# Reordering the end of a two-layer decode block: row sums, mean and squares, a table gelu, one output turn, and a shorter reciprocal square root

## The chip, the core and the metric

The kernel runs on one core of a Trainium2 chip. The core has a matmul engine (PE, TensorE, with weight loads shown apart as PEld), a vector engine (DVE, VectorE), an activation engine (ACT, ScalarE), POOL (GpSimd, nearly unused here) and SP, which does nothing but issue DMA transfers. Each engine executes its own instructions in program order and waits on semaphores of the others. The metric is the device time of one launch in microseconds.

## The reference

Two rounds of attention and feed-forward, with the same weights and the same key and value caches in both rounds. There are 4 batch rows of one token each, 512 wide.

```python
def _A_ref(x, k_cache, v_cache, wq, wo):          # 32 query heads, 8 KV heads, 4096 keys of 128
    q = (x @ wq).reshape(B, Sq, Hq, Dh).transpose(0, 2, 1, 3)
    k, v = jnp.repeat(k_cache, rep, axis=1), jnp.repeat(v_cache, rep, axis=1)
    p = softmax(einsum("bhqd,bhkd->bhqk", q, k) * Dh ** -0.5)
    o = einsum("bhqk,bhkd->bhqd", p, v)
    return o.transpose(0, 2, 1, 3).reshape(B, Sq, Hq * Dh) @ wo
def _B_ref(x, w_gate, w_up, w_down):              # 512 -> 1792 -> 512, gelu in its tanh form
    return (gelu(x @ w_gate) * (x @ w_up)) @ w_down

x = A_x
x = x + _A_ref(layernorm(x), k, v, wq, wo);  x = x + _B_ref(layernorm(x), wg, wu, wd)
x = x + _A_ref(layernorm(x), k, v, wq, wo);  x = x + _B_ref(layernorm(x), wg, wu, wd)
```

Everything is bf16 in memory. Keys and values of one batch row are 8 MB each.

## The kernel before

The second round of a batch row needs the first round's result of that row only, so the kernel goes row by row: the keys of row b are loaded once and used by both rounds, the values twice (but for two tiles that are kept). All transfers are issued from SP (`dq`). Keys lie in eight buffers of two halves (`KT`), values in seven buffers of 512 KB (`free`) that `load_v` refills as steps give them back.

The order of the work is written out by hand (`manual_schedule`); a call is an instruction at that place of its engine's stream. `attend(b2, b1, ...)` interleaves the second round of row b2 with the first round of row b1. `scores` multiplies q with a key half, `soft` is the softmax, `Values.step` is one value step: 16 matmuls of a value tile with the probabilities, after which the buffer goes back. Behind the scores of the second round the keys of the next row are loaded into the same buffers (L530 to L540), so those loads wait for the scores. `attend_last` is the same for the second round of the last row alone: its value steps, parts of the output projection (`out_proj`) between them, then `y_rows` and `y_select`, which turn the projection's row sums and bring them into columns in a PSUM tile that `out_proj_end` adds to.

Between two `attend` calls stands the feed-forward of the first round, `dense`, for one row: `add_y` (residual), `ln_square` and `ln_center` (a matmul with a matrix of 1/512 gives mean and mean of squares on all partitions; the mean is subtracted), `ln_rstd` (the reciprocal square root on VectorE from an integer start value and two Newton steps), gate and up projections (`ffn_in`) with the 512 wide weights moving, `gelu` (a polynomial on VectorE and a tanh on ScalarE), `gate_up`, and `down`. Then the loop that begins at L708 makes the next norm and q, without the norm's weights: `q_rows`, a turn on VectorE, `q_spread`, and `q_build`, a matmul (`qe`) and a product that writes the operand `qb` of the scores. `fill` is called at fixed places of `dense` and of the loop. For rows 1 to 3 it is a value step of the row before; for row 0 there are none, and it issues idle matmuls (`keep_clock`, L342, into a scores bank) in the numbers of a list, in order of the calls:

```python
            waits = iter((1, 5, 6, 2, 1, 0, 3, 1))
            fill = lambda n: keep_clock(next(waits, 0))
```

The first five numbers belong to `dense`'s calls and to the one between `ln_square` and `ln_center` (L716); then one behind `ln_center`, one behind `q_spread` (L726), one behind `q_build` (L728). Later calls find the list empty and issue nothing.

The second round's feed-forward is made once for all four rows, at the very end (from L745), with the weights standing and 4 columns moving: norm, gate in two halves, `gelu` of each half, up in two halves, `down` (4 columns repeated to 32), the residual into `xo`, four 32x32 turns into `xr`, and the store.

Of the kernel before, what the change touches and what calls it, by code (L numbers as in the profile page):

```python
# [15 lines left out]
P = 128  # L16
# [14 lines left out]
def kernel(  # L31
# [67 lines left out]
    OT2_bf = state.tile([P, Hq, B], BF16, name="OT2_bf")  # L99
    q1_bf = state.tile([P, NG, NK, B], BF16, name="q1_bf")  # L100
    xn_bf = state.tile([P, KD, B], BF16, name="xn_bf")
    xo = state.tile([P, QS], BF16, name="xo")
    xr = state.tile([QS, P], BF16, name="xr")
    qb = state.tile([P, W + NK * 2 * W], BF16, name="qb")

    ROWS = [ps_row.tile([P, 512], FP32, name=f"rows{i}") for i in range(2)]
# [1 line left out]
    ident_bf = const.tile([P, P], BF16, name="ident_bf")  # L108
    mean_f = const.tile([P, P], FP32, name="mean_f")
    magic = const.tile([P, B], I32, name="magic")  # L110
    s32_f = const.tile([P, QS], FP32, name="s32_f")
    t32_bf = const.tile([P, QD, QS], BF16, name="t32_bf")
    amask = const.tile([P, QD], FP32, name="amask")
# [28 lines left out]
    def build_consts():  # L142
        nc.vector.memset(mean_f[:], 1.0 / D)
        nc.vector.memset(magic[:], 0x5F3759DF)
        for r in ROWS:
            nc.vector.memset(r[:], 0.0)
        nc.vector.memset(qb[:], 0.0)
        nc.vector.memset(xo[:], 0.0)
        nc.vector.tensor_reduce(out=amask[:], in_=ident_bf[:].rearrange("p (a i) -> p a i", a=QD),
                                axis=AX.X, op=ALU.max)  # L150
        nc.vector.tensor_reduce(out=s32_f[:], in_=ident_bf[:].rearrange("p (a i) -> p i a", a=QD),
                                axis=AX.X, op=ALU.max)
        nc.vector.tensor_copy(out=t32_bf[:],
                              in_=s32_f[:].unsqueeze(1).broadcast_to([P, QD, QS]))
        nc.vector.tensor_reduce(out=hmask[:], in_=s32_f[:].rearrange("p (y h) -> p h y", h=rep),
                                axis=AX.X, op=ALU.max)
        nc.vector.scalar_tensor_tensor(
            out=dmask[:], in0=amask[:].unsqueeze(2).broadcast_to([P, GH, rep]), scalar=float(D),
            in1=hmask[:].unsqueeze(1).broadcast_to([P, GH, rep]), op0=ALU.mult, op1=ALU.mult)
# [11 lines left out]

    def ln_center(b0, nb):
        bs = slice(b0, b0 + nb)
        mv = small.tile([P, 2, nb], FP32, name="mv", tag="mv")
        if nb == 1:
            st = ps_sm.tile([P, 2, 1], FP32, name="st", tag="sm")
            nc.tensor.matmul(st.rearrange("p s o -> p (s o)"), lhsT=mean_f[:, :], rhs=sums[:],
                             start=True, stop=True)
            nc.vector.tensor_scalar(out=xn_bf[:, :, b0], in0=XX[:, 0, b0], scalar1=st[:, 0],
                                    scalar2=None, op0=ALU.subtract)  # L180
            nc.vector.tensor_copy(out=mv[:], in_=st[:])
            return mv
        st = ps_sm.tile([P, 2, nb, KD], FP32, name="st", tag="sm")
        nc.tensor.matmul(st[:], lhsT=mean_f[:, :], rhs=XX[:, :, bs], start=True, stop=True)
        nc.vector.tensor_reduce(out=mv[:], in_=st[:], axis=AX.X, op=ALU.add)
        nc.vector.tensor_tensor(out=xn_bf[:, :, bs].rearrange("p k b -> p b k"), in0=XX[:, 0, bs],
                                in1=mv[:, 0].unsqueeze(2).broadcast_to([P, nb, KD]),
                                op=ALU.subtract)
        return mv

    def ln_rstd(nb, mv):
        msq = small.tile([P, nb], FP32, name="msq", tag="msq")
        nc.vector.tensor_tensor(out=msq[:], in0=mv[:, 0], in1=mv[:, 0], op=ALU.mult)
        var = small.tile([P, nb], FP32, name="var", tag="var")
        nc.vector.scalar_tensor_tensor(out=var[:], in0=mv[:, 1], scalar=LN_EPS, in1=msq[:],
                                       op0=ALU.add, op1=ALU.subtract)
        hv = small.tile([P, nb], I32, name="hv", tag="hv")
        nc.vector.tensor_single_scalar(out=hv[:], in_=var[:].bitcast(I32), scalar=1,
                                       op=ALU.arith_shift_right)
        rstd = small.tile([P, nb], FP32, name="rstd", tag="rstd")  # L200
        nc.vector.tensor_tensor(out=rstd[:].bitcast(I32), in0=magic[:, :nb], in1=hv[:],
                                op=ALU.subtract)
        r2 = small.tile([P, nb], FP32, name="r2", tag="r2")
        for _it in range(2):
            nc.vector.tensor_tensor(out=r2[:], in0=rstd[:], in1=rstd[:], op=ALU.mult)
            nc.vector.scalar_tensor_tensor(out=r2[:], in0=r2[:], scalar=-0.5, in1=var[:],
                                           op0=ALU.mult, op1=ALU.mult)
            nc.vector.scalar_tensor_tensor(out=rstd[:], in0=r2[:], scalar=1.5, in1=rstd[:],
                                           op0=ALU.add, op1=ALU.mult)
        return rstd  # L210
# [110 lines left out]
    def gelu(nb, hg, rstd, sq, h):  # L321
# [6 lines left out]
        nc.scalar.activation(out=sq[:], in_=sq[:], func=ACT.Tanh, scale=GELU_C)  # L328
        nc.vector.scalar_tensor_tensor(out=h[:], in0=h[:], scalar=0.5,
                                       in1=spread_rstd(rstd, n, nb), op0=ALU.mult, op1=ALU.mult)  # L330

    def ffn_tiles(nb):
        sq = small.tile([P, KF, nb], FP32, name="sq", tag="sq")
        h = small.tile([P, KF, nb], FP32, name="h", tag="h")
        return sq, h, small.tile([P, KF, nb], BF16, name="H_bf", tag="H_bf")

    def gate_up(hu, sq, h, H_bf):
        nc.vector.scalar_tensor_tensor(out=sq[:], in0=sq[:], scalar=1.0, in1=h[:],
                                       op0=ALU.add, op1=ALU.mult)
        nc.vector.tensor_tensor(out=H_bf[:], in0=hu, in1=sq[:], op=ALU.mult)  # L340

    def keep_clock(n):  # L342
        if n:
# [2 lines left out]
            nc.tensor.matmul(idle, lhsT=ident_bf[:, :], rhs=wq_sb[0][:, 0, :512],  # L346
                             start=True, stop=True, skip_group_check=True)

    def down(nb, H_bf, between=()):
        n = WIDE * rep // nb  # L350
        y = ps_sm.tile([P, KD, n, nb], FP32, name="y", tag="sm")
        for c in range(KF):
            if c in between:
                keep_clock(between[c])
            for k in range(KD):
                nc.tensor.matmul(y[:, k], lhsT=wd_sb[:, c, k * P:(k + 1) * P],  # L356
                                 rhs=H_bf[:, c, :].unsqueeze(1).broadcast_to([P, n, nb]),
                                 start=(c == 0 and k == 0), stop=(c == KF - 1), skip_group_check=True)
        return y[:, :, 0]


    class Keys:
# [97 lines left out]
        n = early[b]  # L460
        order += value_order(b, 1)[:n] + value_order(b + 1, 0) + value_order(b, 1)[n:]
    order += value_order(B - 1, 1)
    keep = {(0,) + u[2:] for u in value_order(0, 1)[:KEEP]}
    VB = Hkv * NT
    loads = [u for u in order if not (u[1] and (u[0],) + u[2:] in keep)]
    free = [kvin.tile([P, CH, Dh], BF16, name=f"v{i}") for i in range(KV_BUFS)]
# [178 lines left out]
    def attend_last(b2, next_q, rest):  # L645
# [25 lines left out]
        vals.step(4)  # L671
        soft_turn(p0)
        prob2[gb] = (soft_swap(p0, p2p), soft_recip(soft_den(p0)))
        out_proj(rows, OT2_bf, heads[0], hp, True)
        vals.step(5)
        out_proj(rows, OT2_bf, heads[1], hp)
# [3 lines left out]
        out_proj(rows, OT2_bf, heads[4], rep, False, True)  # L680
        yc = y_rows(rows, B)
        vals.step()
        y = y_select(yc, B)
        vals.step()
        return y, OT2_bf, heads[5], rep

    def dense(b0, nb, proj, fill, between=()):
# [1 line left out]
        y = proj[0]  # L689
        fill(1)  # L690
        add_y(b0, nb, y)
        ln_square(b0, nb)
        mv = ln_center(b0, nb)
        fill(1)
        rg = ffn_in(b0, nb, wg_sb)
        fill(1)
# [1 line left out]
        rstd = ln_rstd(nb, mv)  # L698
        sq, h, H_bf = ffn_tiles(nb)
        gelu(nb, ffn_cols(rg, nb), rstd, sq, h)  # L700
        gate_up(ffn_cols(ru, nb), sq, h, H_bf)
        fill(2)
        add_y(b0, nb, down(nb, H_bf, between))

# [3 lines left out]
    for b in range(B):  # L708
# [3 lines left out]
        else:  # L712
            fill = prev.step
        dense(b, 1, proj, fill, {KF // 2: 1, KF - 4: 1} if prev is None else ())
        ln_square(b, 1)
        fill(1)  # L716
        mv = ln_center(b, 1)
        fill(1)
        ga, gb = groups(b + 1)
        qr0 = q_rows(b, 1, ga)  # L720
# [17 lines left out]
    def ffn_part(w_sb, h, c0, c1):  # L738
        for c in range(c0, c1):
            for k in range(KD):  # L740
# [3 lines left out]

    out_proj_end(*proj)  # L745
    add_y(0, B, proj[0])
    ln_square(0, B)
    mv = ln_center(0, B)
    banks = [new_rows(), new_rows()] + [new_scores(i).rearrange("p c j -> p (c j)")
                                        for i in range(NG)]  # L750
    hg, hu = [[t[:, :KF * B].rearrange("p (c j) -> p c j", j=B) for t in banks[i::2]]
              for i in range(2)]
    parts = [(0, KF // 2), (KF // 2, KF)]
    rstd = ln_rstd(B, mv)
    for i, (c0, c1) in enumerate(parts):
        ffn_part(wg_sb, hg[i], c0, c1)
    sq, h, H_bf = ffn_tiles(B)
    for i, (c0, c1) in enumerate(parts):
        gelu(B, hg[i][:, c0:c1], rstd, sq[:, c0:c1], h[:, c0:c1])
    for i, (c0, c1) in enumerate(parts):  # L760
        ffn_part(wu_sb, hu[i], c0, c1)
        gate_up(hu[i][:, c0:c1], sq[:, c0:c1], h[:, c0:c1], H_bf[:, c0:c1])
    y = down(B, H_bf)
    nc.vector.tensor_tensor(out=xo[:, :B * KD].rearrange("p (b k) -> p b k", k=KD),
                            in0=XX[:, 0], in1=y.rearrange("p k b -> p b k"), op=ALU.add)
    for a in range(QD):
        nc.vector.transpose(out=xr[:, a * QS:(a + 1) * QS], in_=xo[a * QS:(a + 1) * QS, :])
    nc.sync.dma_start(out=out.flatten_outer_dims().rearrange("b (k c) -> (b k) c", k=KD),
                      in_=xr[:B * KD, :])


# [28 lines left out]
```

## Time and profile before

| | us |
|---|---|
| median of 3 runs (lowest, highest) | 310.05 (305.14, 310.78) |
| the profiled execution | 310.05 |
| its span, first to last instruction | 308.3 |
| PE busy, in the span | 203.1 |
| DVE busy | 172.0 |
| ACT busy | 29.1 |

Loads move 114.09 MB, at a mean of 370 GB/s. The chain of work that ended last is 55% transfers, 19% PE, 12% DVE and 9% SP's issues. In the views, a row of the order of time has its start, its duration, engine, line, operation, what is written from what is read, the sizes, and in brackets the idle time before it with what ended it. The granted PE clock is given as a share of full speed; in this execution its mean is 0.738, and it is always either 0.5 or 1.0.

### The profile page before, as it was taken

To read this page: it belongs to the slowest core of one execution; us is meant where nothing else is said; L and a number is where in the kernel's file an instruction comes from. 1 tells how busy PE (TensorE), PEld (TensorE's weight loads), DVE (VectorE), ACT (ScalarE), POOL (GpSimd) and SP (SyncE) were. 2 spreads that over 40 slices of the span, in tenths; PEclk is the share of its full clock that TensorE was granted. 3 is DMA by queue.
4 is the path that set the end of the run, shared out by engine and by line. 5 is a ranking of instruction groups with operands and counts; after the bars stand their busy time and mean duration, and the time that the engine had idled before them with its cause. 6 is when DMAs were issued, how large, how long until landed. Compare 5 with 4: busy or idle time off the path is not lost.

```text
span 308.3 us, 8779 instructions
## 1 busy us (share of the span) xinstructions
PE 203.1 (66%) x3873; PEld 119.6 (39%) x3873; DVE 172.0 (56%) x490; ACT 29.1 (9%) x71; POOL 0.7 (0%) x6
## 2 busy tenths in 40 slices
PE   1344285358796649779856379888752787987874
PEld 0012144122324134546431246463511355645654
DVE  6586821014358796545578944344799542555144
ACT  0003001000002020300100212000202030003000
POOL 0000000000000000000000000000000000000000
PEclk9997565556779555989965575877895579798675
DMA  6999999999949999999999999999999999999910
GB/s 247 433 408 426 409 423 410 357 379 385 399 133 367 403 413 418 330 373 415 416 416 406 416 416 392 339 410 376 406 408 410 417 418 318 416 417 417 412 49 3
DMA packets 34558, 114.09 MB, mean 370 GB/s; under 512 B 3156, under 2 KB 9048, under 8 KB 33496
## 3 DMA queue, kind: packets, MB, share of 16 engines
q1 hardware_dynamic: 34520, 113.53, 94.1%
q8 instruction: 30, 0.49, 0.6%
q14 instruction: 8, 0.07, 0.1%
HBM read 113.51 MB, written 0.00 MB: 368 GB/s over the span
## 4 chain that ended last, share of the span: by engine, by line
DMA 55%; PE 19%; DVE 12%; SPq 9%; issue 3%; ACT 2%; DVEq 0%; ACTq 0%
DMA v<-in_A_v_cache_dram 26%; DMA kt<-in_A_k_cache_dram 24%; PE sc L399 4%; PE ot L501 3%; DMA wd_sb<-in_B_w_down_dram 3%; SPq L140 3%; SPq L134 3%; DVE kt L388 3%; PE y L356 3%; DMA kt<-in_A_v_cache_dram 3%; PE rows L314 2%; PE rows L233 2%; PE rows L288 1%; DVE rows L223 1%; DVE pp L426 1%
## 5 line engine op out<-in xcount | busy, mean ns | idle before, releaser
L501 PE MATMUL ot<-pe,v 128*128 128x32 bf16 x1920 | 64.2, 182 | 23.9 <-DMA v<-in_A_v_cache_dram 22.4
L501 PEld LDWEIGHTS <-v 128*128 128x128 bf16 x1920 | 58.2, 101 | 51.3 <-DMA v<-in_A_v_cache_dram 31.1
L388 DVE STREAM_TRANSPOSE kt<-kt 128x1024 f32<-128x1024 f32 x64 | 75.1, 1216 | 3.4 <-DMA kt<-in_A_k_cache_dram 3.2
L399 PE MATMUL sc<-kt,qb 128*32 128x512 bf16 x512 | 54.9, 491 | 19.2 <-DVE kt L388 15.8
L223 DVE STREAM_TRANSPOSE rows<-rows 128x512 f32<-128x512 f32 (+1 forms) x23 | 16.3, 707 | 32.9 <-PE rows L233 14.7
L399 PEld LDWEIGHTS <-qb 128*32 128x32 bf16 x512 | 16.5, 108 | 45.2 <-issue 19.1
L509 DVE TENSOR_TENSOR OT_bf<-ot,rden 128x8 bf16<-128x8 f32 (+1 forms) x40 | 6.6, 164 | 38.1 <-PE ot L501 37.8
L418 ACT ACTIVATE pp<-sc,nm 128x512 bf16<-128x512 f32 x16 | 11.0, 688 | 150.0 <-DVE junk L414 139.4
L445 PE MATMUL x<-pp,ident_bf 128*32 128x128 bf16 x256 | 8.3, 262 | 20.8 <-DVE pp L426 20.8
L288 PE MATMUL rows<-wo_sb,OT_bf 128*1 128x512 bf16 (+1 forms) x136 | 13.9, 505 | 7.3 <-DMA wo_sb<-in_A_wo_dram 6.3
L405 DVE TENSOR_REDUCE m<-sc 128x1 f32<-128x512 f32 x16 | 10.8, 677 | 11.9 <-PE sc L399 11.9
L233 PE MATMUL rows<-wq_sb,xn_bf 128*1 128x512 bf16 (+1 forms) x160 | 14.1, 481 | 4.7 <-DMA wq_sb<-in_A_wq_dram 4.4
L445 PEld LDWEIGHTS <-ident_bf 128*32 128x32 bf16 x256 | 6.1, 113 | 26.0 <-issue 23.9
L346 PE MATMUL sc<-wq_sb,ident_bf 128*128 128x512 bf16 x33 | 13.3, 489 | 0.0
L426 DVE STREAM_TRANSPOSE pp<-pp 128x512 bf16<-128x512 bf16 x16 | 11.2, 699 | 3.6 <-ACT pp L418 3.6
L448 ACT CAST pe<-x 128x512 bf16<-128x512 f32 x16 | 9.4, 585 | 22.4 <-PE x L445 22.4
L356 PE MATMUL y<-H_bf,wd_sb 128*128 128x32 bf16 x280 | 9.6, 192 | 2.6 <-DMA wd_sb<-in_B_w_down_dram 1.5
L254 PE MATMUL qe<-qm,t_bf 128*128 128x64 bf16 x16 | 3.3, 208 | 11.7 <-DVE qm L244 8.4
L356 PEld LDWEIGHTS <-wd_sb 128*128 128x128 bf16 x280 | 8.9, 99 | 3.9 <-DMA wd_sb<-in_B_w_down_dram 2.4
L257 DVE TENSOR_TENSOR qb<-qe,amask 128x256 bf16<-128x256 f32 x16 | 6.8, 424 | 4.6 <-PE qe L254 4.6
L301 DVE SCALAR_TENSOR_TENSOR XX<-XX,y 128x4 f32<-128x4 f32 x8 | 1.3, 158 | 13.3 <-PE y L356 9.4
L436 DVE RECIPROCAL rden<-den 128x16 f32<-128x16 f32 x16 | 4.0, 250 | 8.0 <-PE den L431 7.5
(83 smaller groups left out, 134.1 us busy)
## 6 DMA issues: line engine op xcount, KB each, us to landing
v<-in_A_v_cache_dram SPq DMA_DIRECT2D x117, 512.0 KB, 8.5
kt<-in_A_k_cache_dram SPq DMA_DIRECT2D x48, 512.0 KB, 10.1
kt<-in_A_k_cache_dram SPq DMA_DIRECT2D x8, 1024.0 KB, 15.8
wq_sb<-in_A_wq_dram SPq DMA_DIRECT2D x2, 2048.0 KB, 14.1
wo_sb<-in_A_wo_dram SPq DMA_DIRECT2D x4, 1024.0 KB, 11.7
kt<-in_A_v_cache_dram SPq DMA_DIRECT2D x8, 512.0 KB, 10.1
wg_sb<-in_B_w_gate_dram SPq DMA_DIRECT2D x1, 1792.0 KB, 13.5
wu_sb<-in_B_w_up_dram SPq DMA_DIRECT2D x1, 1792.0 KB
```

The lines of the kernel that those rows point to most:

```text
L223: nc.vector.transpose(out=rows[:, :n], in_=rows[:, :n])
L233: nc.tensor.matmul(rows[j * QS:j * QS + nb, :], lhsT=xn_bf[:, k, bs], rhs=w, start=(k == 0), stop=(k == KD - 1))
L288: nc.tensor.matmul(rows[r0:r0 + lhsT.shape[-1], :], lhsT=lhsT, rhs=wo_sb[:, i, :], start=(start and n < QD), stop=(stop and n >= hp - QD))
L346: nc.tensor.matmul(idle, lhsT=ident_bf[:, :], rhs=wq_sb[0][:, 0, :512], start=True, stop=True, skip_group_check=True)
L356: nc.tensor.matmul(y[:, k], lhsT=wd_sb[:, c, k * P:(k + 1) * P], rhs=H_bf[:, c, :].unsqueeze(1).broadcast_to([P, n, nb]), start=(c == 0 an ...
L388: nc.vector.transpose(out=words, in_=words)
L399: nc.tensor.matmul(sc[s * QS:(s + 1) * QS], lhsT=qb[:, w0:w0 + 2 * W], rhs=kt[:, :, be // 2, :, be % 2], start=(t == 0 and be == 0), stop= ...
L405: nc.vector.tensor_reduce(out=m[:], in_=sc.rearrange("p c j -> p (c j)"), axis=AX.X, op=ALU.max)
L418: nc.scalar.activation(out=pp[:], in_=sc[:], func=ACT.Exp, bias=nm[:, 0:1], scale=scale, accum_out=ls[:])
L426: nc.vector.transpose(out=flat, in_=flat)
L445: nc.tensor.matmul(x[a * QS:(a + 1) * QS, s], lhsT=ident_bf[:, s * QS:(s + 1) * QS], rhs=pT[:, a], start=True, stop=True, skip_group_check ...
L501: nc.tensor.matmul(self.ot[:, s % 2], lhsT=v[:, i, :], rhs=rhs, start=(c == 0), stop=(c == C - 1), skip_group_check=True)
```

## The change

- In `attend_last` the last value step moves ahead of `y_select`. A gelu of the two numbers in `sums`, which nobody reads any more, is issued on ScalarE behind the last softmax.
- The end: `ln_end` takes the mean with a matmul of its own, ahead of the squares. The gate is one group of 56 matmuls. gelu is one activation by table over all 56 columns; `h` becomes gelu times rstd, and each half of the up projection is multiplied with it in one instruction. `down` moves 4 columns. The result is added in two halves of the partitions into a tile of 64 partitions, turned with one instruction, and stored in pieces of 32 numbers.
- For one row `ln_rstd` becomes `ln_rstd_one`: it reads the statistics in PSUM, uses two scalar operands per instruction, and has eight instructions where the copy and the chain had eleven.
- For row 0 (`between` not empty, `prev is None`) `ln_mean` takes the place of `ln_square` and `ln_center` in both norms: mean matmul, squares, centering, second matmul. The `fill` between `ln_square` and `ln_center` goes for this row; the list of numbers stays, so the later calls each take the number before theirs.
- In `gelu` the product (1 + tanh) h moves in from `gate_up`, ahead of the turn of the up rows; `H_bf` is written with four equal columns, and `down` repeats those eight times instead of one column 32 times.

```diff
@@ ln_center, nb == 1
-            nc.vector.tensor_copy(out=mv[:], in_=st[:])
-            return mv
+            return st
...
+    def ln_mean(b0):
+        st = ps_sm.tile([P, 1], FP32, name="st", tag="sm")
+        nc.tensor.matmul(st[:], lhsT=mean_f[:, :], rhs=sums[:, 0:1], start=True, stop=True)
+        ln_square(b0, 1)
+        nc.vector.tensor_scalar(out=xn_bf[:, :, b0], in0=XX[:, 0, b0], scalar1=st[:],
+                                scalar2=None, op0=ALU.subtract)
+        st2 = ps_x.tile([P, 1], FP32, name="st2", tag="x")
+        nc.tensor.matmul(st2[:], lhsT=mean_f[:, :], rhs=sums[:, 1:2], start=True, stop=True)
+        return st, st2
+
+    def ln_rstd_one(st):
+        mean, ex2 = st if isinstance(st, tuple) else (st[:, 0], st[:, 1])
...
+        nc.vector.tensor_scalar(out=nv[:], in0=mean, scalar1=mean, scalar2=ex2, op0=ALU.mult,
+                                op1=ALU.subtract)
...
+        nc.vector.tensor_scalar(out=nh[:], in0=nv[:], scalar1=0.5, scalar2=-0.5 * LN_EPS,
+                                op0=ALU.mult, op1=ALU.add)
...
+        nc.vector.tensor_single_scalar(out=hv[:], in_=nh[:].bitcast(I32), scalar=1,
+                                       op=ALU.arith_shift_right)
...
+        nc.vector.tensor_tensor(out=rstd[:].bitcast(I32), in0=magic1[:], in1=hv[:],
+                                op=ALU.subtract)
...
+        for _it in range(2):
+            nc.vector.tensor_scalar(out=r2[:], in0=rstd[:], scalar1=rstd[:], scalar2=nh[:],
+                                    op0=ALU.mult, op1=ALU.mult)
+            nc.vector.tensor_scalar(out=rstd[:], in0=r2[:], scalar1=1.5, scalar2=rstd[:],
+                                    op0=ALU.add, op1=ALU.mult)
...
+    def ln_end(nb):
...
+        nc.tensor.matmul(st[0][:], lhsT=mean_f[:, :], rhs=XX[:, 0], start=True, stop=True)
+        ln_square(0, nb)
+        nc.tensor.matmul(st[1][:], lhsT=mean_f[:, :], rhs=XX[:, 1], start=True, stop=True)
+        nc.vector.tensor_reduce(out=mv[:, 0], in_=st[0][:], axis=AX.X, op=ALU.add)
...
+        nc.vector.tensor_reduce(out=mv[:, 1], in_=st[1][:], axis=AX.X, op=ALU.add)
@@ gelu, gate_up
+        nc.vector.scalar_tensor_tensor(out=sq[:], in0=sq[:], scalar=1.0, in1=h[:],
+                                       op0=ALU.add, op1=ALU.mult)
...
-    def gate_up(hu, sq, h, H_bf):
-        nc.vector.scalar_tensor_tensor(out=sq[:], in0=sq[:], scalar=1.0, in1=h[:],
-                                       op0=ALU.add, op1=ALU.mult)
-        nc.vector.tensor_tensor(out=H_bf[:], in0=hu, in1=sq[:], op=ALU.mult)
+    def gate_up(hu, sq, H_bf):
+        copies = list(H_bf.shape)
+        nc.vector.tensor_tensor(out=H_bf[:], in0=hu.broadcast_to(copies),
+                                in1=sq[:].broadcast_to(copies), op=ALU.mult)
@@ attend_last
+        nc.scalar.activation(out=sums[:], in_=sums[:], func=ACT.Gelu_apprx_tanh)
...
         vals.step()
+        vals.step()
         y = y_select(yc, B)
-        vals.step()
@@ dense
-        ln_square(b0, nb)
-        mv = ln_center(b0, nb)
+        if between:
+            mv = ln_mean(b0)
+        else:
+            ln_square(b0, nb)
+            mv = ln_center(b0, nb)
@@ the loop over rows
-        ln_square(b, 1)
-        fill(1)
-        mv = ln_center(b, 1)
+        if prev is None:
+            mv = ln_mean(b)
+        else:
+            ln_square(b, 1)
+            fill(1)
+            mv = ln_center(b, 1)
@@ the end
-    for i, (c0, c1) in enumerate(parts):
-        gelu(B, hg[i][:, c0:c1], rstd, sq[:, c0:c1], h[:, c0:c1])
-    for i, (c0, c1) in enumerate(parts):
-        ffn_part(wu_sb, hu[i], c0, c1)
-        gate_up(hu[i][:, c0:c1], sq[:, c0:c1], h[:, c0:c1], H_bf[:, c0:c1])
-    y = down(B, H_bf)
...
+    nc.vector.tensor_tensor(out=h[:], in0=hg, in1=rs, op=ALU.mult)
+    nc.scalar.activation(out=sq[:], in_=h[:], func=ACT.Gelu_apprx_tanh)
+    nc.vector.tensor_tensor(out=h[:], in0=sq[:], in1=rs, op=ALU.mult)
+    for u, c0 in zip(hu, (0, KF // 2)):
+        c1 = c0 + KF // 2
+        ffn_part(wu_sb, u, c0, c1)
+        nc.vector.tensor_tensor(out=H_bf[:, c0:c1], in0=u[:, c0:c1], in1=h[:, c0:c1], op=ALU.mult)
+    y = down(B, H_bf, wide=False)
+    hp = P // 2
+    for i in range(2):
+        ps = slice(i * hp, (i + 1) * hp)
+        nc.vector.tensor_tensor(
+            out=xo.rearrange("p (b k i) -> p i b k", k=KD, i=2)[:, i],
+            in0=XX[ps, 0], in1=y[ps].rearrange("p k b -> p b k"), op=ALU.add)
+    nc.vector.transpose(out=xr[:], in_=xo[:])
```

## The prediction

> **What bounds the kernel now.** I read the page's slices first, to see where the transfers stand still, then the waits of the transfer queue (SP), then the order of time inside the two places found.
>
> ```profile
> PEclk9997565556779555989965575877895579798675
> GB/s 247 433 408 426 409 423 410 357 379 385 399 133 367 403 413 418 330 373 415 416 416 406 416 416 392 339 410 376 406 408 410 417 418 318 416 417 417 412 49 3
> ```
>
> ```profile
> SPq L381 <- PE sc L399: 14.2, 9, 8.9
> ```
>
> A slice is 308.3/40 = 7.7 us. Most move 400 to 418 GB/s: 113.5 MB at 417 would take 272 us, so the loads bound nearly everything. Two places are not bound by them: slice 12 (133 GB/s, 84.8 to 92.5 us) and the last two (49 and 3). The line of the queue's waits (engine and line, who was waited for, total us, times, longest) says what slice 12 is: the next batch's K loads (L381) wait up to 8.9 us for the scores (L399) that free their buffers. Only work in such places can move the end; the rest lies under full transfers. First place, in order of time:
>
> ```profile
> 82.40 0.56 PE L177 MATMUL st<-sums,mean_f 128*128 128x2 f32 x2
> ...
> 83.28 1.88 PE L233 MATMUL rows<-wq_sb,xn_bf 128*1 128x512 bf16 x16 [0.33 <-DVE mv L181]
> ...
> 85.09 1.46 PE L346 MATMUL sc<-wq_sb,ident_bf 128*128 128x512 bf16 x3
> ...
> 86.44 0.23 PE L254 MATMUL qe<-qm,t_bf 128*128 128x64 bf16 x1
> ...
> 86.61 0.58 PE L346 MATMUL sc<-wq_sb,ident_bf 128*128 128x512 bf16 x1
> 86.71 0.42 DVE L257 TENSOR_TENSOR qb<-qe,amask 128x256 bf16<-128x256 f32 x1 [0.33 <-PE qe L254]
> ...
> 87.19 1.69 PE L399 MATMUL sc<-kt,qb 128*32 128x512 bf16 x16
> ...
> 88.90 7.28 SPq L381 DMA_DIRECT2D kt<-in_A_k_cache_dram  x10
> ```
>
> Columns: start, us, engine, line, what. The L346 rows are the idle matmuls of `keep_clock`. Three run while VectorE works on q, one while it builds `qb`; then the scores start. Second place, the end:
>
> ```profile
> 295.94 0.26 PE L276 MATMUL y<-yc,s_f 128*32 128x16 f32 x8 [0.52 <-DVE yc L269]
> 296.13 0.57 PE L501 MATMUL ot<-pe,v 128*128 128x32 bf16 x16
> ...
> 296.95 0.56 PE L294 MATMUL y<-OT_bf,wo_sb 128*128 128x4 bf16 x16 [0.26 <-DVE OT_bf L509]
> 297.55 0.17 DVE L305 TENSOR_TENSOR XX<-XX,y 128x16 f32<-128x16 f32 x1 [0.65 <-PE y L294]
> ...
> 301.08 0.19 DVE L323 TENSOR_TENSOR h<-rows,rstd 128x28 f32<-128x28 f32 x1
> ...
> 301.74 0.23 ACT L328 ACTIVATE sq<-sq 128x28 f32<-128x28 f32 x1 [14.91 <-DVE sq L326]
> ...
> 303.14 1.66 PE L356 MATMUL y<-H_bf,wd_sb 128*128 128x32 bf16 x56 [0.81 <-DVE H_bf L340]
> ...
> 304.83 0.17 DVE L764 TENSOR_TENSOR xo<-XX,y 128x16 bf16<-128x16 f32 x1 [1.36 <-PE y L356]
> 305.03 0.84 DVE L767 STREAM_TRANSPOSE xr<-xo 32x32 bf16<-32x32 bf16 x4
> 305.90 0.35 SPq L768 DMA_DIRECT2D out_dram<-xr  x1
> ```
>
> From 296 us everything is one chain, most of it VectorE instructions about 0.2 us apart, so each one removed counts in full.
>
> **The change, part by part: the end.** Times are of the profiled execution, 310.05 us with a span of 308.27, so 1.8 us lie around the span; its time equals the median of the three runs.
>
> *Row sums behind the last V step.* TensorE runs in order, so the last V step (296.13) now waits for `y_select` (295.94), which waits for VectorE's turn. The transfers have ebbed away at about 295.7, so with the order swapped the step can start near 295.8, and `y_select` runs while VectorE scales the result. Gain 0.3.
>
> *Mean ahead of squares.* Normalised values come about 0.2 earlier, but the gate projection they feed (56 matmuls, 1.5 us) ends before `rstd` is there anyway. What counts is `rstd`: before, `add_y` at 297.55, one statistics matmul, `rstd` used at 301.08, which is 3.53 later. After: the mean matmul starts about 0.3 behind `add_y`, the second statistics matmul follows it on TensorE (two times about 0.55, the L184 row has 0.61 for both sums), a second reduce (0.19), then the same ten instructions at 0.2: about 3.6. Loss 0.1. The shorter chain is only for one row; this one has four and keeps its ten.
>
> *Table gelu.* From 301.08 to 303.14 (2.06 us) stand two halves of h, two polynomial steps, tanh, and their tail. After: h at 128x56 (0.25; the 28-wide rows take 0.19 to 0.22), one activation (0.26, from the 0.23 row), h times rstd (0.25), the first up product (0.2), and three handovers of about 0.05: 1.05 to 1.1. The up projection's first half is done by then (gate and up are 1.5 + 0.75 us of matmuls behind xn). Gain 1.0.
> Here a rule speaks against the change: the Trainium skill, "ScalarE: Activation LUTs", section "Table sets: the hidden batching unit", has exp and tanh in one set and gelu in another, and asks that calls be grouped by set. This trace's one table load took 1.28 us (25.68), and the page puts a switch at 2.66 with its drain. Left on the chain that would turn the 1.0 gain into a loss of 0.3 or 1.7. But the load is issued behind the last softmax copy of ScalarE (about 287), nothing else is queued behind it, and the tanh row shows 14.91 us idle. I take nothing for it.
>
> *Down projection with 4 columns, not 32.* 56 in 1.66 us are 29.6 ns each; the 4-column gate matmuls ran 28 in 0.74, 26.5 ns each. Gain 0.15, none if its weight loads (56 in 1.54) set the pace.
>
> *Output.* Add 0.17 and four turns 0.84 with gaps make 1.07. After: two adds on half the partitions (0.17 and, not dependent on it, 0.1 to 0.2) and one turn (0.2): 0.6. Gain 0.47. The store becomes 64 pieces of 64 bytes instead of 16 of 256, four to a transfer engine in place of one; its packets are of some 20 ns, so I put 0.1 against it (0 to 0.3).
>
> Sum at the end: 0.3 - 0.1 + 1.0 + 0.15 + 0.47 - 0.1 = 1.7 us gained.
>
> **The middle layers.** Each of the eight one-row norms loses three of its eleven VectorE instructions (0.195 apart, so 0.6), and one more, the 0.19 of (1+tanh)h, moves ahead of the second turn; the `H_bf` product grows from 14 to 56 columns (+0.04). For batches 1 and 3 (134 to 154, 262 to 276 us) the transfers run at 400 to 420 GB/s throughout: nothing. For batch 2 the K loads are issued at 213.2 behind such a chain, and 209 to 213 us runs at 300 to 360 GB/s, some 0.75 us of transfer lost. I take half, 0.4 (0 to 0.75).
>
> **The first q block.** Up to 81.17 it waits for the last `wd_sb` load, which covers all that is saved ahead of it in batch 0. Behind that there are three edits. The filler in front of the statistics matmul goes, and the mean no longer waits for the square: the mean starts about 0.2 sooner. A second statistics matmul (0.5 at half clock, 0.3 at full) and one filler (0.43 or 0.22) then stand between it and `q_rows`. And since one call of `fill` is gone while the list of counts is unchanged, the counts slide: no filler where three were, three where one was (behind `qe`, in front of the scores), one more in the second block.
> At half clock, as in this profile: mean 82.2 to 82.76, second sum to 83.27, filler to 83.75, `q_rows` 1.88 to 85.6, turn and `qm` to 86.6, `qe` to 86.9, three fillers to 88.25, where `qb` would have been ready at 87.4. The scores start 1.05 later. At full clock `q_rows` takes 1.1 and is not the bound: the shorter rstd chain (three instructions off, but started 0.2 later behind the second sum) gains 0.35, three fillers of 0.22 fit nearly under `qb` (0.42): a gain of 0.2. The transfers idle there, so either passes to the end.
> The Trainium skill, "TensorE: Matmul & The Clock Gate", section "The HAM clock gate", has the clock change only at the edges of free-running windows of 3.4 us, whose place against the kernel differs from run to run; the half-clock stretch 81.6 to 88.5 in this trace is two such windows. By the row of this one execution the block costs 1.05; by the rule it is as often the other. I take the middle, +0.4.
>
> **Sum.** 310.05 - 1.7 - 0.4 + 0.4 = 308.3 us.
>
> **Rivals.** *Slower:* the fillers in front of the scores. Besides the 1.05, TensorE then idles about a microsecond before `qe`, the window to 88.5 may no longer count as busy, and the next 3.4 us (full clock in this profile) run at half: the second `q_rows` 1.88 instead of 1.08 and the scores of the second half 1.7 instead of 1.04, some 1.6 more. Transfers run at only 205 to 240 GB/s there, so it passes on: +2.7 - 2.1 = 310.6. It decides once the K issue is later by over 2.1 us. For it: the half clock in the profile; against: it needs one phase of the window.
> *The lower pattern:* one of the three runs took 305.14, with no change in the program; with 1.7 off it, 303.4. For it: the spread of 5.6 us is larger than the whole sum, and half-clock stretches are all over the profile. Against: two of three runs lie at 310.
> *It does not do what it says:* a step such as the table load or the second sum lands on the chain after all, and the end gains under half a microsecond: 309.8.
>
> **How the numbers follow.** The main case 0.5 (307.3 to 309.1 by its own bounds), slower 0.13, the lower pattern 0.25, no gain 0.12. The range 303.2 to 310.9 leaves out some 0.15. Faster by over 2% means below 303.85, which only the lower pattern reaches, and not all of it: 0.15. Slower by over 2% (316.25) needs something that no view shows: 0.02. Two per cent, 6.2 us, is about what a measurement of this kernel can tell from no change; all of the sum lies inside.
>
> **What would show it.** Right: between the start of the last add into XX and the first down matmul about 4.7 us instead of 5.6; a table load near 287 and one gelu activation with no load before it; from the last down matmul to the store's issue 0.6; three L346-type fillers behind `qe`, and the K issue some 6.5 to 9 us behind the last `wd_sb` landing (7.8 now). Wrong: K loads over 2 us later against that landing, a gap of transfers that is new in batches 1 to 3, or a tail over 12 us behind the last V matmuls.

## The result, and the profile after

| | before | changed |
|---|---|---|
| median of all runs, us | 308.62 (32 runs, 303.70 to 311.69) | 308.69 (27 runs, 306.19 to 312.74) |
| mean of all runs | 308.40 | 309.01 |
| profiled execution, its span | 310.05, 308.3 | 308.33, 306.6 |

The ratio of changed to before is 1.0074, with a 95% interval of 1.0050 to 1.0098. That ratio leaves out each kernel's runs over 1.5% above its own lowest, and one very low run of before (303.70) makes it leave out 17 of before's 32, so it overstates the loss. Beside each ratio I therefore give the difference of the means of all runs with a resampled 95% interval, here +0.61 us (-0.29 to +1.56): no gain, and perhaps a small loss. The forecast was a gain of 1.75. The base of the forecast, a median of three runs (310.05), was a high sample: with 32 runs before stands at 308.6.

In the profiled pair the changed kernel is 1.7 us shorter, just what was forecast. That is luck: one pair, out of runs of each kernel that spread over 6 to 8 us. But its end looks as it was meant to. The order of time of the changed kernel, at its end (start, duration, engine, line, what):

```profile
285.61 1.28 ACT L726 ACT_TABLE_LOAD   x1
...
296.15 0.57 PE L344 MATMUL y<-OT_bf,wo_sb 128*128 128x4 bf16 x16
...
296.76 0.17 DVE L355 TENSOR_TENSOR XX<-XX,y 128x16 f32<-128x16 f32 x1 [0.66 <-PE y L344]
...
300.18 0.22 DVE L813 TENSOR_TENSOR h<-rows,rstd 128x56 f32<-128x56 f32 x1
300.43 0.25 ACT L814 ACTIVATE sq<-h 128x56 f32<-128x56 f32 x1 [13.33 <-DVE h L813]
...
301.28 1.64 PE L408 MATMUL y<-H_bf,wd_sb 128*128 128x4 bf16 x56
302.95 0.35 DVE L824 TENSOR_TENSOR xo<-XX,y 64x16 bf16<-64x16 f32 x2 [1.51 <-PE y L408]
303.34 0.20 DVE L827 STREAM_TRANSPOSE xr<-xo 64x32 bf16<-64x32 bf16 x1
303.57 0.63 SPq L828 DMA_DIRECT2D out_dram<-xr  x1
```

From the last add into `XX` to the first down matmul it is 301.28 - 296.76 = 4.52 us, where before had 303.14 - 297.55 = 5.59. From the start of down to the store's issue it is 2.29 for 2.76. The table load lies in ScalarE's idle time: the gelu finds ScalarE idle for 13.33 us.

What the sum had no term for is in the page's slices, clock and transfer rate of the changed kernel:

```profile
PEclk9999997556958957957985558579855597798655
...
GB/s 254 428 411 427 404 410 405 350 371 392 383 153 317 406 411 408 407 407 402 394 404 407 410 407 406 407 388 322 399 408 413 408 408 407 408 407 406 408 119 3
```

Before, the slices 32, 33 and 35 to 37 stood at 416 to 418; here they stand at 406 to 408. That is no gap at one place but a lower rate wherever values stream. A stretch with nothing but value loads, 174 to 184 us, shows it best. The transfers of that stretch, in before:

```profile
DMA packets 1143, 4.17 MB, mean 417 GB/s; under 512 B 127, under 2 KB 127, under 8 KB 1142
```

and in the changed kernel:

```profile
DMA packets 1111, 4.06 MB, mean 406 GB/s; under 512 B 122, under 2 KB 122, under 8 KB 1110
```

The transfer engines are busy throughout in both, with the same kind of packet, but 3% fewer pass. By the trace's packet records a 4096-byte packet of this stretch takes 159.5 ns on average before and 163.3 after. Values are 117 loads of 512 KB, 61.3 MB: 147.0 us at 417 GB/s, 151.0 at 406. Were all of it at these rates, 4 us would be lost (an estimate), more than the whole forecast gain.

### The profile page after: what moved, and what is told of

The parts are those of the page before. It is cut to its first block, busy times and chain, and to the rows that moved or that the text cites. A ratio compares the mean times of both kernels' runs of the same rounds, so it can differ in the third digit from the quotient of the medians.

```text
span 306.6 us, 8755 instructions
## 1 busy us (share of the span) xinstructions
PE 201.9 (66%) x3879; PEld 118.6 (39%) x3879; DVE 171.1 (56%) x458; ACT 30.6 (10%) x72; POOL 0.7 (0%) x6
## 4 chain that ended last, share of the span: by engine, by line
DMA 59%; PE 18%; DVE 10%; SPq 9%; issue 2%; ACT 0%; DVEq 0%
DMA v<-in_A_v_cache_dram 33%; DMA kt<-in_A_k_cache_dram 20%; PE ot L553 4%; PE sc L451 3%; DMA kt<-in_A_v_cache_dram 3%; SPq L135 3%; DMA wd_sb<-in_B_w_down_dram 3%; SPq L141 3%; PE rows L364 3%; PE y L408 2%; DVE rows L273 2%; PE sc L398 1%; PE rows L283 1%; SPq L136 1%; SPq L427 1%
## 5 line engine op out<-in xcount | busy, mean ns | idle before, releaser
L553 PE MATMUL ot<-pe,v 128*128 128x32 bf16 x1920 | 65.6, 182 | 25.0 <-DMA v<-in_A_v_cache_dram 23.0
L451 PE MATMUL sc<-kt,qb 128*32 128x512 bf16 x512 | 53.6, 479 | 18.3 <-DVE kt L440 16.2
L497 PE MATMUL x<-pp,ident_bf 128*32 128x128 bf16 x256 | 7.6, 246 | 19.3 <-DVE pp L478 19.3
L408 PE MATMUL y<-H_bf,wd_sb 128*128 128x32 bf16 (+1 forms) x280 | 8.4, 176 | 2.1 <-DMA wd_sb<-in_B_w_down_dram 1.6
L408 PEld LDWEIGHTS <-wd_sb 128*128 128x128 bf16 x280 | 7.8, 98 | 3.5 <-DMA wd_sb<-in_B_w_down_dram 2.7
L283 PEld LDWEIGHTS <-xn_bf 128*1 128x1 bf16 (+1 forms) x160 | 3.8, 91 | 9.7 <-issue 6.3
```

The source lines that it names most:

```text
L283: nc.tensor.matmul(rows[j * QS:j * QS + nb, :], lhsT=xn_bf[:, k, bs], rhs=w, start=(k == 0), stop=(k == KD - 1))
L451: nc.tensor.matmul(sc[s * QS:(s + 1) * QS], lhsT=qb[:, w0:w0 + 2 * W], rhs=kt[:, :, be // 2, :, be % 2], start=(t == 0 and be == 0), stop= ...
L497: nc.tensor.matmul(x[a * QS:(a + 1) * QS, s], lhsT=ident_bf[:, s * QS:(s + 1) * QS], rhs=pT[:, a], start=True, stop=True, skip_group_check ...
L553: nc.tensor.matmul(self.ot[:, s % 2], lhsT=v[:, i, :], rhs=rhs, start=(c == 0), stop=(c == C - 1), skip_group_check=True)
```

## The experiments

None of the kernels leaves work out. The first four were made while it was open which part takes the gain back: the list of filler counts, the front, the end or the store. The others test what the first four pointed at, the placement of the load buffers. Ratio and difference are against before, measured together.

**List of filler counts moved** (changed kernel, one number taken out so that the counts stand where they stood):

```diff
-            waits = iter((1, 5, 6, 2, 1, 0, 3, 1))
+            waits = iter((1, 5, 6, 2, 0, 3, 1))
```

> The changed kernel with the list of idle matmuls moved up by one place, so that three again run in front of qe and one behind it. Theory A (the end gains about 1.4 us as the changed profile shows, and the slid idle matmuls in front of the scores of the first q block give it back): 1 to 1.5 us below the changed kernel's mean, so about 0.5 to 1 below the kernel before. Theory B (the end itself does not gain, for the store of small pieces and the second statistics matmul cost what the rest saves): as the changed kernel, within 0.3. K issue behind the last wd_sb landing: A 7.3 us, against 8.1 in the changed kernel.

Ratio 1.0030 (0.9998 to 1.0061), difference +0.10 (-0.76 to +1.03), 22 runs. The keys' issue came 7.77 us behind the last `wd_sb` matmul's start instead of 8.07. The mean is 0.4 below that of the changed kernel (0.5 above to 1.2 below), where theory A asked for 1 to 1.5: a part of the loss may lie here, hardly the whole.

**Only the end** (before with `ln_end`, the table gelu and its early load, row sums behind the last V step, 4-column down, new output):

```diff
-    ln_square(0, B)
-    mv = ln_center(0, B)
+    mv = ln_end(B)
...
-    xr = state.tile([QS, P], BF16, name="xr")
+    xr = state.tile([P // 2, QS], BF16, name="xr")
```

> The kernel before with the edits of the end alone: attend_last, ln_end, the table gelu, the narrow down and the output turn. Theory A: 1.4 us below the kernel before (-0.45%). Theory B: within 0.3 of the kernel before, or above it.

Ratio 1.0053 (1.0021 to 1.0084), difference +0.72 (-0.27 to +1.75), 22 runs. The gain of theory A did not come: the end alone, with its chain visibly shorter (4.52 us from the last add into `XX` to the first down matmul, as in the changed kernel), gains nothing. And its values stream at 409 GB/s, though no load was touched.

**Only the front** (the changed kernel with before's end):

```diff
-    mv = ln_end(B)
+    ln_square(0, B)
+    mv = ln_center(0, B)
...
-    xr = state.tile([P // 2, QS], BF16, name="xr")
+    xr = state.tile([QS, P], BF16, name="xr")
```

> The changed kernel with the end undone: only ln_mean, the slid list, the shorter rstd chain, the moved product and the four columns of H_bf are left. Theory A: 1.4 to 2 us above the kernel before. Theory B: within 0.5 of the kernel before.

Ratio 1.0107 (1.0044 to 1.0171), difference +2.10 (+0.85 to +3.40), 6 runs; values at 408 GB/s. Either half of the change lowers the rate. They have no edit of an instruction in common, so one cause in both would be something else that they share.

**The old output in the changed kernel** (one add, four turns, 16 pieces of 256 bytes, and the old sizes of `xo` and `xr`):

```diff
...
-    nc.vector.transpose(out=xr[:], in_=xo[:])
+    for a in range(QD):
+        nc.vector.transpose(out=xr[:, a * QS:(a + 1) * QS], in_=xo[a * QS:(a + 1) * QS, :])
...
```

> The changed kernel with the old output: one add, four turns, a store of 16 pieces of 256 bytes. The turns cost 0.45 more; in the changed profile 3.0 us lie between the store's issue and the end of the span, against 2.4 before, so the store costs 0.65 less. Theory A: 0.2 below the changed kernel (no difference that can be measured). Theory B: 0.6 or more below it.

Ratio 1.0064 (1.0034 to 1.0095), difference +0.10 (-0.63 to +0.80), 22 runs; values at 409 GB/s. From the store's issue to the end of the unrounded span 2.38 us, as before (2.37), against 2.98 with 64 pieces of 64 bytes. In the profiles, then, the store gives back what the output edit gains on VectorE. The mean is 0.4 below that of the changed kernel (1.1 below to 0.3 above), which doesn't tell theory A (0.2) from theory B (0.6).

**What both halves share** is size. I take it that the tiles of SBUF are laid out one behind the other, rounded to 32 bytes per partition: constants, weights and keys, state, then the value buffers. `magic1` then adds 32 bytes ahead of the weights, the narrower `xr` takes 192 away ahead of the values. Sizes give only differences of place, so I also take before's value buffers to start at a multiple of 256 bytes. Then they start 96 off in the changed kernel, 64 off in the end alone, 32 off in the front alone and in the kernel with the old output. Both assumptions are tested by the pads below, which were computed from them. The cheapest test changes no instruction at all.

**Before, values moved by 96 bytes:**

```diff
-    xr = state.tile([QS, P], BF16, name="xr")
+    xr = state.tile([QS, P + 48], BF16, name="xr")[:, :P]
```

> The kernel before with 96 unused bytes behind xr, so that the value buffers start 96 bytes off a multiple of 256; not an instruction is changed. Theory C: value packets at 163 to 164 ns, time 1.5 to 2.5 us above the kernel before (+0.5 to 0.8%). Theory A: no change at all.

Ratio 1.0093 (1.0062 to 1.0123), difference **+2.06** (+1.08 to +2.97), 22 runs. The transfers of 174 to 184 us in this kernel:

```profile
DMA packets 1117, 4.08 MB, mean 408 GB/s; under 512 B 125, under 2 KB 125, under 8 KB 1116
...
v<-in_A_v_cache_dram SPq DMA_DIRECT2D x7, 512.0 KB, 8.3
```

and its page's slices:

```profile
GB/s 246 428 410 424 406 409 406 351 373 392 383 175 309 413 409 408 406 404 372 397 408 407 409 408 408 406 385 367 405 410 409 407 408 408 408 405 408 395 39 3
```

Before's instructions with the changed kernel's rate (405 to 408 in the slices where before had 416 to 418), and a time to match.

**Before unchanged, profiled on the same chip as that one:**

> The kernel before, unchanged, for a profile from the same chip as the others. Theory C: 4096-byte packets of the value stretches at about 160 ns here as in the first profile. If the difference between the profiles came from the chip: 163 to 164, as in the other kernels' profiles.

309.26 us; the stretch again as in the first profile of before, so it is not the chip:

```profile
DMA packets 1143, 4.17 MB, mean 417 GB/s; under 512 B 127, under 2 KB 127, under 8 KB 1142
```

**The changed kernel, values back on 256 bytes** (measured twice, under two names):

```diff
-    xr = state.tile([P // 2, QS], BF16, name="xr")
+    xr = state.tile([P // 2, QS + 80], BF16, name="xr")[:, :QS]
```

> The changed kernel with 160 unused bytes behind xr, so that the value buffers v0 to v6 start at a multiple of 256 bytes again, as they did in the kernel before (they start 96 bytes off in the changed kernel, since xr shrank by 192 bytes and magic1 takes 32). Theory C (the end gains what was forecast, and the value loads lose more than that, for their destination is no longer aligned: 4096-byte packets in value stretches took 163.7 ns in the changed profile and 159.7 in the one before): packets back at about 160 ns, and the time 1.5 to 2.5 us below the changed kernel, about 1.5 below the kernel before. Theory A (the slid idle matmuls alone): as the changed kernel, packets too, or the time within 0.3.

> The changed kernel with 160 unused bytes behind xr, value buffers at multiples of 256 bytes as in the kernel before. If alignment is the only thing the forecast missed: 1.2 to 1.8 us below the kernel before. If a second cause takes the gain back: equal to it within 0.5.

First 1.0002 (0.9963 to 1.0041), -0.45 (-1.69 to +0.83), 14 runs; then 0.9947 (0.9918 to 0.9977), **-2.22** (-3.09 to -1.29), 22 runs. Weighted by runs, -1.5. The two differ by 1.8 us for one and the same kernel, so differences between sets of measurements are less sure than the intervals say. The rate does not waver: the stretch moves 418 GB/s again in the first and 417 in the second.

```profile
DMA packets 1144, 4.18 MB, mean 418 GB/s; under 512 B 127, under 2 KB 127, under 8 KB 1143
```

**Which part holds that gain:** the same pad with the filler list moved back, and before with the end only, padded to the same place:

```diff
-            waits = iter((1, 5, 6, 2, 1, 0, 3, 1))
+            waits = iter((1, 5, 6, 2, 0, 3, 1))
...
-    xr = state.tile([P // 2, QS], BF16, name="xr")
+    xr = state.tile([P // 2, QS + 80], BF16, name="xr")[:, :QS]
```

```diff
-    xr = state.tile([P // 2, QS], BF16, name="xr")
+    xr = state.tile([P // 2, QS + 96], BF16, name="xr")[:, :QS]
```

> The same with the list of idle matmuls moved up by one place. If the slid list costs 0.7 on average (the K issue behind the last wd_sb landing was 7.9 us in profiles with the slid list and 7.2 without): 0.7 below h1, about 2.2 below the kernel before. If the list counts for nothing: as h1.

> The kernel before with the edits of the end alone and 192 unused bytes behind xr, so that the value buffers are aligned as before. The end's gain in the profiles is 0.9 to 1.2: that much below the kernel before, where the same edits without the bytes were 0.7 above it. If the end's gain does not reach the time: equal to the kernel before.

List moved: 0.9929 (0.9897 to 0.9962), -2.36 (-3.21 to -1.45). End only: 0.9921 (0.9890 to 0.9952), -2.40 (-3.27 to -1.53). 22 runs each. The end alone holds all of the gain; with the rest of the change the mean is 0.2 higher (0.9 lower to 1.3 higher), nothing that can be told from zero. Against the end alone with its values 64 bytes off (+0.72, measured on another chip), 192 unused bytes are worth 3.1 us (1.8 to 4.5).

**Everything on 256 bytes.** By the same sizes weights and keys were 160 off before and 192 off in the changed kernel, so they can be moved too:

```diff
-    magic1 = const.tile([P, 1], I32, name="magic1")
+    magic1 = const.tile([P, 23], I32, name="magic1")[:, :1]
...
-    xr = state.tile([P // 2, QS], BF16, name="xr")
+    xr = state.tile([P // 2, QS + 48], BF16, name="xr")[:, :QS]
```

The changed kernel with the list moved, twice:

> The changed kernel with the list of idle matmuls moved up by one place, 160 unused bytes in all ahead of the value buffers, of which 64 lie ahead of the weights, so that weights, key buffers and value buffers all start at multiples of 256 bytes. Theory C: key packets too at about 160 ns instead of 163.5, and the time 3 to 4.5 us below the changed kernel: below both. If alignment counts for nothing: as the changed kernel with the list moved up, about 0.4 below the changed kernel.

> The kernel of f4_list_kv0 once more, beside the three others: 301 to 302.4, and below the aligned kernel before by 2.5 us or more (end 1.2 to 1.4, first q block 0.3 to 0.8, middle layers the rest).

0.9826 (0.9771 to 0.9881), **-6.91** (-8.09 to -5.83), median 301.56; and 0.9826 (0.9778 to 0.9875), -5.51 (-7.15 to -3.66), median 302.78; 6 runs each. It is faster than both kernels. Two stretches of its windows view (window, length, busy us of PE, PEld, DVE, ACT, POOL, granted clock, share of the transfer engines, GB/s): the first holds weights and keys, the second the `wo` rows, which are 1024 bytes long:

```profile
8.00:25.00 17.00, 7.44 (x49) 2.06 (x49) 11.23 (x13) 0.00 (x0) 0.00 (x0) 1.00 1.02 426
54.00:64.00 10.00, 3.93 (x50) 1.28 (x46) 0.16 (x1) 0.00 (x0) 0.00 (x0) 0.50 1.09 387
```

and the same two in before:

```profile
8.00:25.00 17.00, 7.02 (x49) 2.04 (x49) 11.43 (x14) 0.00 (x0) 0.00 (x0) 1.00 1.02 420
54.00:64.00 10.00, 3.26 (x48) 1.54 (x49) 0.16 (x1) 0.00 (x0) 0.00 (x0) 0.50 1.10 355
```

The share of busy is the same, the rate 1.4% and 9% higher.

The same placement for before (the diff), for the changed kernel with its own list, and for the end only:

```diff
-    magic = const.tile([P, B], I32, name="magic")
+    magic = const.tile([P, B + 24], I32, name="magic")[:, :B]
...
-    xr = state.tile([QS, P], BF16, name="xr")
+    xr = state.tile([QS, P + 80], BF16, name="xr")[:, :P]
```

> The kernel before with 96 unused bytes ahead of the weights and 160 behind xr: weights, key and value buffers all start at multiples of 256 bytes; not an instruction is changed. Theory C (alignment of the loads' destinations): weights and key buffers gain what the value buffers have, about 2.3% of some 47 MB, 2.5 to 3 us, and the whole comes to 304.5 to 306. The step from here to the changed kernel with its list moved up and all aligned (301.6) is then what the change is worth: 3 to 4 us. If alignment counts only for the values: 308, as the kernel before.

> The changed kernel, its list of idle matmuls as it is, with weights, key and value buffers at multiples of 256 bytes. Theory C with the forecast's sum: 1.5 to 2 us below the kernel before that is aligned in the same way. Theory A on top of it (slid idle matmuls cost about 1 us): 1 us above the same kernel with the list moved up. If the list counts for nothing: equal to that one.

> The kernel before with the edits of the end alone, all aligned. The end gained 1.1 to 1.4 us in the profiles: 1.1 to 1.4 below the aligned kernel before. If the gain of the end does not reach the time: equal to it.

Before 0.9869 (0.9803 to 0.9934), -3.47 (-5.65 to -1.14); changed 0.9726 (0.9644 to 0.9808, from two of its runs only), -4.91 (-7.95 to -2.04); end only 0.9857 (0.9793 to 0.9922), -3.54 (-5.49 to -1.62). With 6 runs each, all lie below before, and they can't be told from one another: against before at the same placement, the change is worth -1.4 (-4.7 to +1.8) and the end only -0.1 (-2.5 to +2.3).

## Why the prediction was wrong

**The step that failed** is the reading that "the loads bound nearly everything", followed by a sum that took their rate as given. "Only work in such places can move the end" holds for instructions; it does not hold for what sets the rate itself. The change has a term of its own there: one tile resized and one added, 96 bytes at the values' start, measured alone at +2.06. With the gain at equal placement, -1.5 to -2.2, that makes -0.2 to +0.5, each part unsure by about 1 us, and +0.61 (-0.29 to +1.56) was measured. That the gain at equal placement comes near the forecast 1.75 is in part luck, for its terms did not come as forecast (below). The rivals missed the rate as well; "lands on the chain after all" comes nearest to the measured time, for a wrong reason.

Every sign that the prediction named for being right came in: 4.52 us for the 4.7, the table load with no other before the gelu, 0.62 us from the adds behind down to the store's issue, three fillers behind `qe`, the keys' issue at 8.07. None of its signs of being wrong did. All of them watch chains and gaps, and none watches the rate.

The diff showed the two sizes, and a rule pointed at them: the Trainium skill, "DMA: Bandwidth & Descriptors", section "How a descriptor splits into AXI transactions", cuts a transfer into transactions of 256 bytes that must start on 256-byte addresses; with an unaligned start, the bytes from the boundary below it are fetched too and cost beats (of 32 bytes). It words this for what is fetched; what moved here is where the bytes are written. For a 4096-byte row 96 bytes off, that is 17 transactions instead of 16 (6%), or 131 beats instead of 128 (2.3%); for a 1024-byte row 160 off, 5 instead of 4 (25%), or 37 beats instead of 32 (16%). The packets took 163.3 against 159.5 ns (2.4%), and 50.4 against 46.1 to 46.3 ns (9%). As estimates from the page, on the values' 147 us, transactions of equal time would have cost 9.2 us and beats 3.4; measured were 2.06. The direction agrees, and the longer rows suffer less, as the page has it, but neither count gives both sizes. Nor do the beats grow right: 32 bytes off would be one beat more and 192 off six, yet the packets took 163.0 to 163.6 ns at every start but the aligned one. The measurement decides: 3 to 6 ns more for each packet, whatever its length and its place off the boundary. Why, no run here shows. Starts 32, 64, 96, 160 and 192 bytes off were slow; 128 off was not tried, so these runs don't tell a boundary of 256 bytes from one of 128.

**The end, term by term.** Row sums, forecast 0.3: from the last value packet to the add into `XX` 2.0 us on average in five profiles with the old order, 1.7 in twelve with the new; in the profiled pair only 0.05. Mean ahead of squares and gelu, forecast -0.1 and +1.0: together 5.59 - 4.52 = 1.07 (from the add to `h` 3.42 for 3.53, so +0.1 and not -0.1; from `h` to down 1.10 for 2.06). Down with 4 columns, forecast 0.15 or none if weight loads set the pace: 1.66 to 1.64, none. Output, forecast 0.47: 1.07 - 0.62 = 0.45. The store, forecast 0.1 within 0 to 0.3: 2.98 - 2.37 = 0.61, mis-sized; its issue alone went from 0.35 to 0.63, and it ends later behind that. Table load at no cost: right, 1.28 us at 285.6. Sum: 0.3 + 1.07 + 0.02 + 0.45 - 0.61 = 1.2 instead of 1.7. In the runs the end alone gave 2.4 (1.5 to 3.3) with the values placed as before, and 0.1 (-2.3 to +2.5) with everything aligned. The 1.2 lies between; the part of the 2.4 above it is not accounted for.

**The middle layers**, forecast 0.4 from 0.6 per norm: the chain in batch 1 of the changed kernel,

```profile
143.73 0.23 DVE L180 TENSOR_SCALAR xn_bf<-XX,st 128x4 bf16<-128x4 f32 x1 [0.54 <-PE st L178]
143.87 0.28 DVE L206 TENSOR_SCALAR nv<-st 128x1 f32<-128x1 f32 x1
...
144.76 0.28 DVE L219 TENSOR_SCALAR r<-rstd,nh 128x1 f32<-128x1 f32 x1
145.07 0.21 DVE L221 TENSOR_SCALAR rstd<-r,rstd 128x1 f32<-128x1 f32 x1
145.32 0.27 DVE L219 TENSOR_SCALAR r<-rstd,nh 128x1 f32<-128x1 f32 x1
145.63 0.21 DVE L221 TENSOR_SCALAR rstd<-r,rstd 128x1 f32<-128x1 f32 x1
145.88 0.23 DVE L782 TENSOR_SCALAR am<-amask,rstd 128x4 f32<-128x4 f32 x1
```

takes 2.15 us from `xn_bf` to `am`, against 2.27 in before:

```profile
143.72 0.23 DVE L179 TENSOR_SCALAR xn_bf<-XX,st 128x4 bf16<-128x4 f32 x1 [0.54 <-PE st L177]
...
145.01 0.16 DVE L206 SCALAR_TENSOR_TENSOR r<-r,var 128x1 f32<-128x1 f32 x1
145.21 0.16 DVE L208 SCALAR_TENSOR_TENSOR rstd<-r,rstd 128x1 f32<-128x1 f32 x1
...
145.99 0.23 DVE L723 TENSOR_SCALAR am<-amask,rstd 128x4 f32<-128x4 f32 x1
```

It saves 0.12, not 0.6: three instructions fewer, but the new ones with two scalars from memory take 0.27 to 0.28, those with one from memory and a constant 0.21, where the old took 0.16. The duration from the neighbouring rows was the mistake. In batch 2, from whose keys the 0.4 was taken, `xn_bf` to `am` is 2.16 for 2.27. The keys' issue there does come 0.97 earlier (212.22 for 213.19), but 0.78 of that is the clock: the 16 score matmuls ahead of it took 1.11 us at full clock, 1.89 at half before.

**The first q block**, forecast a loss of 0.4 between -0.2 and +1.05:

```profile
83.70 1.66 PE L283 MATMUL rows<-wq_sb,xn_bf 128*1 128x512 bf16 x16
...
86.76 0.21 PE L304 MATMUL qe<-qm,t_bf 128*128 128x64 bf16 x1 [1.40 <-DVE qm L294]
86.78 1.46 PE L398 MATMUL sc<-wq_sb,ident_bf 128*128 128x512 bf16 x3
...
88.18 1.90 PE L451 MATMUL sc<-kt,qb 128*32 128x512 bf16 x16
90.10 7.43 SPq L433 DMA_DIRECT2D kt<-in_A_k_cache_dram  x10
```

The three fillers moved from ahead of `qe` to behind it, as foreseen, and the keys' issue came 8.07 us behind the last `wd_sb` matmul's start (82.03) against 7.73: +0.34 in this pair. Over all profiles it is 6.61 to 8.59 us (mean 8.0) in the six with the slid list, 6.90 to 7.73 (7.2) in the seven with before's front, and 6.50 to 7.77 (6.8) in the four with the list moved back. As a shift it is within the forecast, at twice its middle. What it costs in time the runs can't tell: moving the list back changed the mean by -0.14 (-1.2 to +0.9). The slower rival, an issue later by over 2.1 us, was in no profile.

**Still open:** how much of the last 3 to 4 us belongs to the weights' and how much to the keys' placement, and whether the list matters once all is placed. An estimate from the number of packets and what each lost gives 2.2 us for the weights and 2.3 for the key buffers, if every packet lay on the path.

## What to carry to other kernels

When loads bound a kernel, compare the steady rate of transfers in both profiles before looking at any chain: 3% of rate outweighed 1.2 us of chain. A change that resizes or adds a small tile moves every buffer allocated behind it, so place load destinations on 256 bytes on purpose, as all the fast runs here had them, and compare two versions only at equal placement. Two halves of a change that lose in the same way are a sign of something that both share and neither states. And let one of the signs that a prediction is to be judged by watch the resource that it takes as given.

## What the runs showed of the hardware

Start of the destination in SBUF, modulo 256 bytes, worked out as above. In stretches of full transfers, rows of 4096 bytes take 159.0 to 159.8 ns a packet where it is 0, and 163.0 to 163.6 where it is 32, 64, 96, 160 or 192. For weights and the first keys, aligned against 160 or 192 off: rows of 8192 bytes 309.5 against 313.8 to 314.5; rows of 3584 bytes 140.0 to 140.5 against 145.4 to 145.8; rows of 1024 bytes 46.1 to 46.3 against 50.2 to 51.1. So a long row does not escape the price; it only spreads it over more bytes.

The down matmuls of the middle layers moved one column 32 times before and four equal columns 8 times after. This row of before

```profile
204.26 1.92 PE L356 MATMUL y<-H_bf,wd_sb 128*128 128x32 bf16 x56
```

is 34 ns each, and this of the changed kernel

```profile
204.52 1.57 PE L408 MATMUL y<-H_bf,wd_sb 128*128 128x32 bf16 x56
```

28 ns. Both ran at full clock but for the first 0.26 us of before's. It lies under full transfers, and I count nothing for it.
